# A linear attention followed by two MLPs on one core: a written-out order for the opening and the first block, and three chunks' y written from ScalarE's queue

## The chip, the core and the metric

One core of a Trainium2 chip runs the whole program. The metric is the device time in microseconds (us) of one execution. TensorE (PE) multiplies matrices into the eight PSUM banks, VectorE (DVE), ScalarE (ACT) and GpSimd (POOL) work element by element, and DMAs move data between HBM and SBUF. Every engine takes its own instructions in a fixed order and waits on semaphores for the others; a DMA is issued from the queue of an engine too, here always from SyncE's (SP) before the change.

## The reference, cut to what matters

```
B, H, S, D = 4, 8, 768, 48
for t in range(S):                                   # per batch and head
    state = alpha[t][:, None] * state + outer(k[t], v[t])
    y[t]  = q[t] @ state
x = y as (3072 tokens, 384)
x = (h * sigmoid(1.702 * h)) @ w_out,    h = x @ w_in        # 384 -> 2048 -> 384
x = (h - tanh(h)) @ w2_out,              h = x @ w2_in       # the same sizes
```

The weights of the MLPs come as 64-bit floats and are turned into pairs of 32-bit numbers on the chip.

## The kernel before, in words

**Attention.** Tokens go in 24 chunks of 128 (six per batch). A chunk g is loaded by four or five DMAs (`a_load`), its decays are multiplied up by two scans on DVE (`a_scan`), its queries and keys are scaled by two DVE multiplications (`a_scale`), and then PE makes the scores in two halves (`a_scores`, L273: two halves of four heads), ACT copies them out of PSUM (L278, L286), POOL cuts them to the causal triangle (L283), and PE makes the output y (`a_out`: L302 what the state carries, L305 what the chunk's own scores give) and the change of the state (L312), which DVE adds up (L316, L317, L319). `a_guard` squares the decays on ACT for a check at the end. For the first eight chunks (`FULL = 8`) the triangle is POOL's and the scaling DVE's; for the later ones the triangle is DVE's mask and the scaling POOL's.

**From y to x.** `a_evac` copies y out of PSUM on ACT (L326), writes it to HBM with four DMAs (L331) and reads it back in another layout with one (L332), after which ACT rounds it to `xhi` (L333) and DVE (or POOL) takes the rest as `xlo` (L334).

**The MLPs.** Each runs in 6 blocks of 512 tokens, 16 steps m to a block. A step is nine matmuls of `gemm1` (L343), the activation (`sig_1`: ACT L357, DVE L358), a split of the result into two (`g_split`: ACT L361, DVE or POOL L362) and, three steps later, nine matmuls of `gemm2` (L350). The hidden values alternate between banks 3 and 4, so `gemm1` of step m+2 overwrites what `sig_1` of step m reads. The first block of the first MLP needs chunks 0 to 3, and beside it chunks 4 to 7 are computed, and so on: every block of the first MLP but the last carries four chunks of the next.

**Weights.** A weight tile m is loaded as 64-bit words into one of three buffers `raw` (L153), and converted by DVE in `w_bits` (L160, L161), `w_join` (L173) and `w_split` (ACT's copy L190, DVE's L191). `conv` takes one step of a pipeline of three tiles: it splits one, joins the next and takes the bits of the one after, and the load of tile m+3 follows the join of tile m, whose buffer it takes. In the first block of the first MLP every step needs a tile that has been converted.

**The order.** The program is written as a list and a scheduler, which has a model of the engines' times, reorders it and fixes each engine's order at build time. Nothing ties the opening's order before the change.

**What the change touches:** `a_out` (L289), `a_evac` (L321), `conv` (L416), `attend` (L440), the opening (L455 to L475), and in the main loop the part for the first block (L493 to L511).

## Time and profile before

| | us |
|---|---|
| median of three runs | 974.35 (973.78 to 976.83) |
| the profiled execution | 975.3 |
| its span on the core | 973.2 |
| PE busy | 940.9 (97%) |
| DVE busy | 606.0 (62%) |
| ACT busy | 460.6 (47%) |
| POOL busy | 191.7 (20%) |

Times in the profile are counted from the start of the span; between that span and the profiled execution's own time lie 2.1 us outside it. "Busy" of PE counts matmuls whose ends are modelled and overlap, so that 97% doesn't mean that PE runs at its best. The granted share of TensorE's clock stands in the tables by stage; a matmul of 512 columns every 0.23 us is the clock's upper level (2.4 GHz), and one every 0.43 us the lower (1.2 GHz).

### The profile page before, as it was taken

Reading aid. Unit: us, or ns where it says so; the run is one execution under the profiler, and the core shown is the slowest. Engines: PE = TensorE matmul, PEld = TensorE weight load, DVE = VectorE, ACT = ScalarE, POOL = GpSimd, SP = SyncE. Lnnn points to the kernel's source line nnn. Section 1 sums busy time; section 2 is a strip of 40 time slices with the busy share of each in tenths; the row PEclk is TensorE's granted clock in tenths of the full one; section 3 lists DMA queues with packets and bytes.
Section 4 is the critical chain, followed back from the end, with each engine's and each line's share of the span. In section 5 each row is a group of like instructions: output and inputs, shape, how many; then the busy total and the mean of one; then the engine's idle time right before and its main releaser. Section 6 shows DMA issues by size and latency. Waiting matters only on the chain.

```text
span 973.2 us, 13227 instructions
## 1 busy us (share of the span) xinstructions
PE 940.9 (97%) x4870; PEld 739.7 (76%) x4870; DVE 606.0 (62%) x914; ACT 460.6 (47%) x969; POOL 191.7 (20%) x150
## 2 busy tenths in 40 slices
PE   5968999999999999999999999999999999999997
PEld 4646787777777777777788888888888888888885
DVE  7989742442343453453339996766777777766663
ACT  4445434333443534434344555554556656545542
POOL 1222202434434434334230110100100101000000
PEclk9999999999999999999999999999999999999999
DMA  9795221432445463761324330100233420000001
GB/s 282 245 305 166 85 53 28 131 92 67 137 141 153 151 205 116 247 196 41 92 71 158 134 130 1 65 33 0 70 126 98 161 100 0 33 1 1 33 0 37
DMA packets 58043, 101.84 MB, mean 105 GB/s; under 512 B 4992, under 2 KB 37376, under 8 KB 57968
## 3 DMA queue, kind: packets, MB, share of 16 engines
q1 hardware_dynamic: 57968, 100.90, 32.6%
q8 instruction: 40, 0.66, 0.3%
q14 instruction: 35, 0.29, 0.1%
HBM read 86.73 MB, written 14.16 MB: 104 GB/s over the span
## 4 chain that ended last, share of the span: by engine, by line
PE 87%; DMA 5%; DVE 5%; issue 1%; ACT 1%; SPq 0%; POOL 0%; DVEq 0%; ACTq 0%
PE bank L350 40%; PE bank L343 40%; DMA arena<-xq 4%; PE bank L273 3%; PE bank L305 2%; DMA raw<-w 2%; DVE arena L237 1%; PE bank L302 1%; PE bank L312 1%; DVE cf L161 1%; DVE cf L173 1%; DVE wlo L191 0%; DVE cf L160 0%; DVE xs L173 0%; ACT arena L248 0%
## 5 line engine op out<-in xcount | busy, mean ns | idle before, releaser
L343 PE MATMUL bank<-xhi,whi 128*128 128x512 f32 x576 | 230.0, 400 | 0.2 <-ACT xhi L333 0.2
L343 PE MATMUL bank<-xlo,whi 128*128 128x512 f32 x576 | 229.8, 399 | 0.0
L343 PE MATMUL bank<-xhi,wlo 128*128 128x512 f32 x576 | 229.0, 398 | 0.0
L350 PE MATMUL bank<-ghi,whi 128*128 128x512 f32 x576 | 229.0, 398 | 0.0
L350 PE MATMUL bank<-ghi,wlo 128*128 128x512 f32 x576 | 228.5, 397 | 0.0
L350 PE MATMUL bank<-glo,whi 128*128 128x512 f32 x576 | 223.8, 396 | 0.0
L361 ACT CAST ghi<-gt 128x512 fp32r<-128x512 f32 x192 | 119.0, 620 | 199.2 <-DVE gt L373 124.1
L358 DVE SCALAR_TENSOR_TENSOR gt<-gt,bank 128x512 f32<-128x512 f32 x96 | 65.5, 682 | 125.8 <-ACT gt L357 122.7
L362 DVE TENSOR_TENSOR glo<-gt,ghi 128x512 fp32r<-128x512 f32 x128 | 93.2, 728 | 79.4 <-ACT ghi L361 76.0
L343 PEld LDWEIGHTS bank<-xhi,whi 128*128 128x128 f32 x576 | 109.0, 189 | 27.4 <-issue 1.6
L343 PEld LDWEIGHTS bank<-xlo,whi 128*128 128x128 f32 x576 | 109.1, 189 | 26.2 <-issue 1.4
L343 PEld LDWEIGHTS bank<-xhi,wlo 128*128 128x128 f32 x576 | 109.2, 190 | 25.7 <-issue 0.6
L350 PEld LDWEIGHTS bank<-ghi,whi 128*128 128x128 f32 x576 | 108.5, 188 | 26.4 <-issue 1.2
L350 PEld LDWEIGHTS bank<-ghi,wlo 128*128 128x128 f32 x576 | 108.5, 188 | 25.4 <-issue 0.8
L350 PEld LDWEIGHTS bank<-glo,whi 128*128 128x128 f32 x576 | 108.3, 188 | 25.1 <-DVE arena L243 0.2
L362 POOL TENSOR_TENSOR glo<-gt,ghi 128x512 fp32r<-128x512 f32 x64 | 85.8, 1341 | 139.0 <-ACT ghi L361 127.8
L410 POOL TENSOR_TENSOR xlo<-arena,xhi 128x512 fp32r<-128x512 f32 x18 | 27.9, 1574 | 307.6 <-ACT xhi L409 307.6
L357 ACT ACTIVATE gt<-bank 128x512 f32<-128x512 f32 x96 | 57.1, 595 | 64.0 <-PE bank L343 63.1
L237 DVE TENSOR_TENSOR_SCAN arena<-arena,seg 112x516 f32<-112x516 f32 x46 | 62.8, 1365 | 35.4 <-DMA arena<-xq 34.7
L371 DVE SCALAR_TENSOR_TENSOR arena<-arena,bank 128x512 f32<-128x512 f32 x96 | 65.7, 685 | 30.4 <-ACT arena L369 29.7
L369 ACT ACTIVATE arena<-bank 128x512 f32<-128x512 f32 x96 | 57.3, 597 | 42.2 <-PE bank L343 41.9
L373 DVE SCALAR_TENSOR_TENSOR gt<-arena 128x512 f32<-128x512 f32 x96 | 68.3, 711 | 9.4
(85 smaller groups left out, 853.7 us busy)
## 6 DMA issues: line engine op xcount, KB each, us to landing
raw<-w SPq DMA_DIRECT2D x64, 768.0 KB, 4.7
arena<-xq SPq DMA_DIRECT2D x46, 224.0 KB, 3.0
arena<-xq SPq DMA_DIRECT2D x22, 451.5 KB, 5.8
xt<-arena SPq DMA_DIRECT2D x96, 48.0 KB, 3.0
xlo<-xt SPq DMA_DIRECT2D x24, 192.0 KB, 4.1
x1t<-xs SPq DMA_DIRECT2D x6, 768.0 KB, 5.2
arena<-x1t SPq DMA_DIRECT2D x6, 768.0 KB, 4.6
out<-xs SPq DMA_DIRECT2D x18, 256.0 KB, 2.3
```

The costliest lines, as they stand in the source:

```text
L237: V.tensor_tensor_scan(out=dec(g, n), data0=src(g, n), data1=seg, initial=0.0, op0=ALU.mult, op1=ALU.max)
L273: P.matmul(out=o[hh][:, i], lhsT=k[r, 2 * x + i], rhs=q[r, 2 * x + i], start=True, stop=True)
L343: P.matmul(out=h, lhsT=w[m][:, ws], rhs=x[:, k, :n], start=c == 0, stop=c == 3 * KT - 1)
L350: P.matmul(out=acc[k][:, :n], lhsT=w[m][:, ws], rhs=x[s % 3][:, :n], start=m == 0 and c == 0, stop=m == MT - 1 and c == 2)
L357: A.activation(out=th[i][:, :n], in_=h, func=AF.Tanh, scale=0.851)
L358: V.scalar_tensor_tensor(out=gf[i][:, :n], in0=th[i][:, :n], scalar=1.0, in1=h, op0=ALU.add, op1=ALU.mult)
L361: A.copy(ghi[s % 3][:, :n], gf[s % 2][:, :n])
L362: e.tensor_tensor(out=glo[s % 3][:, :n], in0=gf[s % 2][:, :n], in1=ghi[s % 3][:, :n].bitcast(F32), op=ALU.subtract)
L369: A.activation(out=u, in_=h, func=AF.Square, accum_out=usum[:, s - NS1 :][:, :1])
L371: V.scalar_tensor_tensor(out=p, in0=u, scalar=P3, in1=h, op0=ALU.mult, op1=ALU.mult)
L373: V.scalar_tensor_tensor(out=gf[i], in0=w, scalar=PD, in1=p, op0=ALU.add, op1=ALU.mult)
L410: G.tensor_tensor(out=xlo[i][:, k], in0=xr[:, k], in1=xhi[i][:, k].bitcast(F32), op=ALU.subtract)
```

## The change

It fixes the order of every engine's instructions (and of every queue's DMAs) from the first one to the end of the first block of the first MLP: `in_order` ties each instruction to the one written before it on the same engine. With that, the list itself is written anew. What moves:

- Loads: chunk 2 goes ahead of weight tiles 0 and 1, chunk 3 and tile 2 come after chunk 0's y, and a weight load is put off (`due`) to a `fetch()` behind the chunk's work.
- The opening runs chunk after chunk: the scores of chunk g, the scans and the scaling of chunk g+1, at most one step of `conv`, then y and the state of chunk g. Five steps of `conv` are taken ahead of the first block.
- The rounding of x (`a_x`) of chunk g comes two chunks later; y and its way back (`a_back`) are apart from it.
- For the first four chunks, `a_out` adds what the state carries after the chunk's own part instead of before it; y lies in banks 0 and 1, the scores in banks 5, 6, 3 and 4.
- y has a second buffer, which shares memory with `wt`. The y of chunks 1, 2 and 3 is written by DMAs from ACT's queue, the others from SP's.
- In the first block, `conv` and the weight load come ahead of the chunk's part of a step and `sig_1` after it; chunk 4+i takes steps 3i, 3i+1 and 3i+2.

```diff
+        early = g < L1[0][1] // C
+        if c and not early:
+            carried(True)
         for p, hh in heads:
...
+        if c and early:
+            carried(False)
...
     def a_evac(g, b):
+        ys = ysb[g % 2 if g < FULL else 0]
...
-                SP.dma_start(out=xt[2 * n + hh :: 4, :, tk].rearrange("h d t -> d h t"), in_=y4[64 * n : 64 * n + D, hh])
+                (A if 0 < g < L1[0][1] // C else SP).dma_start(out=xt[2 * n + hh :: 4, :, tk].rearrange("h d t -> d h t"), in_=y4[64 * n : 64 * n + D, hh])
+        if g >= FULL:
+            a_back(g)
+            a_x(g)
...
+    def a_back(g):
...
         SP.dma_start(out=xl[:, :, o].bitcast(F32), in_=xt.rearrange("h d t -> (h d) t")[:, tk].rearrange("(k p) t -> p k t", p=128))
+
+    def a_x(g):
+        xh, xl, o = a_at(g)
         A.copy(xh[:, :, o], xl[:, :, o].bitcast(F32))
         (V if g < FULL else G).tensor_tensor(out=xl[:, :, o], in0=xl[:, :, o].bitcast(F32), in1=xh[:, :, o].bitcast(F32), op=ALU.subtract)
...
             if m + 3 < MT:
-                w_load(layer, m + 3)
+                due.append((layer, m + 3))
...
+    def a_done(g, b=5):
+        a_evac(g, b)
+        if g + 2 < NG:
+            a_load(g + 2)
+        if g < FULL:
+            a_back(g)
...
+    def in_order(since):
+        last = {}
+        for ins in nc.cur_bb.bb.instructions[since:]:
+            if ins.engine in last:
+                tc.add_manual_dep(ins, last[ins.engine], mybir.DependencyInfo(
+                    mybir.DependencyClass.NoSync, mybir.DependencyReason.DATA), reason="in_order")
+            last[ins.engine] = ins.name
...
     a_load(1)
+    a_load(2)
+    w_load(1, 0)
+    w_load(1, 1)
+    for b in (0, 1, 7):
+        V.memset(bank[b], 0.0)
...
+    for r in range(3):
+        prep(0, r)
+    for g in range(4):
+        if g > 1:
             conv(1)
+        for r in range(2):
+            a_scores(g, r, (5, 3)[r])
+        if g < 3:
+            for r in range(3):
+                prep(g + 1, r)
+        else:
+            prep(4, 0)
+            prep(4, 1)
+        if g == 1:
+            conv(1)
+        if g > 1:
+            a_x(g - 2)
+        a_guard(g)
+        a_out(g, 0)
+        a_state(g)
+        a_evac(g, 0)
+        if g < 2:
+            a_load(g + 3)
+        if g == 0:
+            w_load(1, 2)
+        fetch()
+        a_back(g)
+    conv(1)
+    a_x(2)
+    a_x(3)
+    fetch()
+    a_load(5)
+    conv(1)
+    prep(4, 2)
+    prep(4, 3)
...
-            if l == 1:
+            if l == 1 and j:
                 sig_1(s, h, n)
-            else:
+            elif l == 1:
+                conv(1)
+                fetch()
...
+                    todo = ((4 * (m // 3) + m % 3,) if m % 3 < 2 else (4 * (m // 3) + 2, 4 * (m // 3) + 3)) if m < 12 else ()
+                for r in todo:
                     attend(t1 // C + r // 4, r % 4)
             if l == 1 and j == 0:
-                conv(1)
+                sig_1(s, h, n)
+                if m % 3 == 2 and m < 12:
+                    a_done(m // 3 + 4)
+                    a_state(m // 3 + 4)
+                    prep(m // 3 + 5, 3)
+                if m % 3 == 1 and m > 3:
+                    a_x(m // 3 + 3)
...
+        if s == MT - 1:
+            in_order(begin)
```

## Rows read from the trace of the kernel before

**Rows 1.** Stages: length; busy PE, PEld, DVE, ACT, POOL; clock, DMA share, GB/s.

```profile
0.00:65.50 65.50, 46.33 (x304) 34.34 (x305) 57.29 (x86) 29.17 (x79) 14.20 (x14) 1.00 0.89 274
65.50:83.00 17.50, 13.17 (x63) 9.26 (x63) 17.50 (x28) 9.05 (x21) 2.87 (x2) 0.81 0.81 259
...
150.35:234.01 83.66, 83.66 (x529) 64.62 (x528) 31.48 (x56) 31.83 (x71) 33.63 (x27) 1.00 0.32 92
624.41:691.33 66.92, 66.92 (x289) 54.26 (x288) 46.29 (x65) 34.45 (x70) 4.45 (x4) 1.00 0.10 36
```

**Rows 2.** PE in order of time: the first matmul of block 0, and of block 1.

```profile
65.50 0.80 PE L343 MATMUL bank<-xhi,whi 128*128 128x512 f32 x1 [0.18 <-ACT xhi L333]
...
150.35 0.39 PE L343 MATMUL bank<-xhi,whi 128*128 128x512 f32 x1
```

**Rows 3.** The chain of waits up to 100 us: start, length, what.

```profile
19.95 11.16 DMA arena<-xq
...
45.91 8.71 DMA raw<-w
```

**Rows 4.** PE in order of time in the opening: start, length, instructions.

```profile
8.72 4.05 PE L273 MATMUL bank<-arena 48*128 48x176 f32 x16 [8.72 <-ACT arena L218]
...
21.44 1.55 PE L273 MATMUL bank<-arena 48*128 48x176 f32 x8
...
59.32 1.28 PE L312 MATMUL bank<-arena 128*48 128x48 f32 x16
62.33 1.11 PE L302 MATMUL bank<-arena,state 48*48 48x128 f32 x16 [1.73 <-DVE state L317]
63.37 1.95 PE L305 MATMUL bank<-arena 128*48 128x128 f32 x16
```

**Rows 5.** Groups by line, ACT to 65.4 us, POOL to 110: busy us, mean ns.

```profile
L278 ACT COPY arena<-bank 128x256 f32<-128x256 f32 x20 | 7.6, 378 | 10.1 <-PE bank L305 6.3 <-PE bank L273 3.8
...
L283 POOL TENSOR_SCALAR_AFFINE_SELECT arena<-arena 128x512 f32<-128x512 f32 x14 | 21.7, 1555 | 78.5 <-ACT arena L278 72.2 <-ACT arena L286 6.3
```

**Rows 6.** POOL in order of time: two selects, one after the other.

```profile
44.95 5.60 POOL L283 TENSOR_SCALAR_AFFINE_SELECT arena<-arena 128x512 f32<-128x512 f32 x2 [6.99 <-ACT arena L278]
```

**Rows 7.** SP's queue in order of time: one chunk's y and its read back.

```profile
107.75 1.81 SPq L331 DMA_DIRECT2D xt<-arena  x4
110.92 0.40 SPq L332 DMA_DIRECT2D xlo<-xt  x1
```

**Rows 8.** ACT in order of time: the rounding that waits for that read.

```profile
113.37 0.52 ACT L333 CAST xhi<-xlo 128x384 fp32r<-128x384 f32 x1 [1.51 <-DMA xlo<-xt]
```

**Rows 9.** DVE in order of time, with no idle time between these.

```profile
84.13 1.22 DVE L237 TENSOR_TENSOR_SCAN arena<-arena,seg 112x516 f32<-112x516 f32 x1
85.27 0.53 DVE L160 TENSOR_SCALAR cf<-raw 128x768 int32<-128x768 int32 x1
85.73 0.55 DVE L160 TENSOR_SCALAR xs<-raw 128x768 int32<-128x768 int32 x1
86.19 0.68 DVE L362 TENSOR_TENSOR glo<-gt,ghi 128x512 fp32r<-128x512 f32 x1
86.80 0.67 DVE L358 SCALAR_TENSOR_TENSOR gt<-gt,bank 128x512 f32<-128x512 f32 x1
87.39 0.94 DVE L191 TENSOR_TENSOR wlo<-xs,whi 128x768 fp32r<-128x768 f32 x1
...
88.35 0.66 DVE L243 TENSOR_TENSOR arena<-arena 112x512 f32<-112x512 f32 x1
88.93 0.95 DVE L161 SCALAR_TENSOR_TENSOR cf<-raw,cf 128x768 int32<-128x768 int32 x1
89.80 0.95 DVE L161 SCALAR_TENSOR_TENSOR xs<-raw,xs 128x768 int32<-128x768 int32 x1
```

**Rows 10.** DMA issues up to 66 us: count, KB each, median us to landing.

```profile
raw<-w SPq DMA_DIRECT2D x12, 768.0 KB, 8.1
...
xt<-arena SPq DMA_DIRECT2D x17, 48.0 KB, 4.7
```

More of the change, by code (lines that the diff above doesn't have):

```diff
@@ L82, in linear_attention_mlps @@
     raw = [T(f"raw{i}", (128, WC, 2), I32) for i in range(3)]
-    wt = [T(f"wt{i}", (128, WC), mybir.dt.int16) for i in range(2)]
+    wtb = T("wtb", (128, WC))
+    wt = [wtb[:, i * WC // 2 : (i + 1) * WC // 2].bitcast(mybir.dt.int16) for i in range(2)]
     wsum = T("wsum", (128, 2 * MT))
@@ L296, in at, with carried @@
             return y[hh][64 * (p % 2) : 64 * (p % 2) + D, p // 2]
-        if c:
+        def carried(start):
             for p in range(NP):
@@ L301, in a_out @@
                     r = slice(64 * hh, 64 * hh + D)
-                    P.matmul(out=at(p, hh), lhsT=state[r, p], rhs=q[r, p, :C], start=p < 2, stop=False)
+                    P.matmul(out=at(p, hh), lhsT=state[r, p], rhs=q[r, p, :C], start=start and p < 2, stop=not start and p >= 2)
+        early = g < L1[0][1] // C
+        if c and not early:
+            carried(True)
         for p, hh in heads:
@@ L305, in a_out @@
             P.matmul(out=at(p, hh), lhsT=vt(g)[:, p, D * hh : D * hh + D], rhs=s4[:, hh, p % 2],
-                     start=not c and p < 2, stop=p >= 2)
+                     start=(early or not c) and p < 2, stop=not (c and early) and p >= 2)
+        if c and early:
+            carried(False)
         if c < NCH - 1:
@@ L313, in a_out, with a_state @@
                              start=True, stop=True)
+            if g >= FULL:
+                a_state(g)
+    def a_state(g):
+        c = g % NCH
+        if c < NCH - 1:
+            dl = bank[7][:DP, : NP * D].rearrange("p (a e) -> p a e", a=NP)
             al = dec3(g + 1, 0)[:, :, C:].to_broadcast([DP, NP, D])
@@ L414, in linear_attention_mlps, with fetch @@
     cv = [0, 0, 0]
+    due = []
+    def fetch():
+        while due:
+            w_load(*due.pop(0))
     def conv(layer, split=True):
@@ L443, in attend @@
         if r < 2:
-            a_scores(g, r, (b0, b1)[r])
+            a_scores(g, r, b)
         if r == 2:
-            a_out(g, b0)
-        if r:
+            a_out(g, b)
+        if 0 < r < 3 or r == 3 and g >= FULL:
             prep(g + 1, r)
-        if r == 3:
-            a_evac(g, b0)
-            for n in {0: (3,), 1: (4,), 2: ()}.get(g, (g + 2,)):
-                if n < NG:
-                    a_load(n)
+        if r == 3 and g >= FULL:
+            a_done(g, b)
+    def in_order(since):
[5 more added lines that the diff above has]
+            last[ins.engine] = ins.name
+    begin = len(nc.cur_bb.bb.instructions)
     V.memset(seg, A_MIN)
@@ L506, in linear_attention_mlps @@
                 t1, n1 = L1[j + 1]
-                parts, span = n1 // C * 4, 11
-                for r in range(min(parts, -(-m * parts // span)), min(parts, -(-(m + 1) * parts // span))):
+                if j:
+                    parts, span = n1 // C * 4, 11
+                    todo = range(min(parts, -(-m * parts // span)), min(parts, -(-(m + 1) * parts // span)))
+                else:
+                    todo = ((4 * (m // 3) + m % 3,) if m % 3 < 2 else (4 * (m // 3) + 2, 4 * (m // 3) + 3)) if m < 12 else ()
+                for r in todo:
                     attend(t1 // C + r // 4, r % 4)
             if l == 1 and j == 0:
-                conv(1)
+                sig_1(s, h, n)
[5 more added lines that the diff above has]
+                    a_x(m // 3 + 3)
             if 2 <= j < 4 and m % 2:
```

32 lines of the change are left out of this document (13 added, 19 removed).

## The prediction

> **What bounds the kernel now.** I read the table by stage first. From about 83 us on, PE is busy without a gap; a block of the second MLP, which has nothing but its matmuls, takes 66.92 us, and block 1 of the first MLP, which carries four chunks of attention beside the same matmuls, 83.66 us [rows 1]. So a step of matmuls (half a sixteenth of 66.92, one `gemm` of nine) is 2.09 us, and a chunk costs PE (83.66 - 66.92) / 4 = 4.2 us. From block 1 on PE is the bound, and nothing of the change lies there. The change lies in the first 150.35 us, up to block 1's first matmul [rows 2]. Of these, 65.5 pass before block 0's first matmul, and block 0 takes 84.85, against what PE needs for it: 16 `gemm1`, 13 `gemm2` (the last three fall into block 1) and four chunks, 29 x 2.09 + 16.7 = 77.4 us. So 7.5 us are lost in block 0, and whatever of the 65.5 can be saved comes on top.
>
> Then I asked what bounds the opening. DVE is busy 57.3 of the first 65.5 us and all of the next 17.5, PE 46.3 of the 65.5, and DMA engines 0.89 of it at 274 GB/s [rows 1]. The chain of waits goes through loads that took 11.16 us (a chunk's) and 8.71 us (a weight tile's) [rows 3], because chunks and weight tiles share the bandwidth, and otherwise through DVE's conversions. Those conversions run many weight tiles ahead, while block 0's first matmul needs one tile. So the opening is late because work that could wait stands ahead of work that can't.
>
> **The change part by part.** *The opening's chain.* In the new order PE may start the scores of chunk g+1 only after all of `a_out(g)`. The period of a chunk is then a chain: two halves of scores, 1.55 us each; ACT's two copies of the second half, 2 x 0.38; POOL's select of it, 1.56 in the mean; the chunk's own part of y 1.95, the carried part 1.11, the state's 1.28 [rows 4, 5]. The sum is 9.8, but modelled ends run past the next start (L302 starts at 62.33, L305 at 63.37, which is 1.04 and not 1.11 [rows 4]), with some 0.1 to 0.2 in each of five groups of PE: I take 9.0. Bounds: 8.2 with the select at half its mean, and 10.7 with selects of 2.8 us, as in the pair that took 5.60 [rows 6]. DVE needs less per chunk (next part but one: 3.6 of scans and scaling, at most 3.1 of conversion, 1.0 of smaller ones), so that PE, ACT and POOL's chain sets the pace. The first scores start at 8.72 us [rows 4], which stays: constants and chunk 0 are still the first loads, and two more memsets of DVE fall into its wait for them. Chunk 3's y is complete at 8.72 + 4 x 9.0 - 1.28 = 43.4. From there to x: two copies 0.8, and 5.6 us from the first DMA of y to the rounding (107.75 to 113.37, in a stretch with little traffic [rows 7, 8]). Block 0's first matmul (T0) comes at 43.4 + 0.8 + 5.6 + 0.5 = **50.3**, between 47 and 57, against 65.5. I take 50.
>
> *The loads.* Chunk 2 ahead of tiles 0 and 1, chunk 3 behind chunk 0's y on SP. At 274 GB/s [rows 1], chunks 0 to 2 (1.1 MB each by the sizes of their arrays) and two tiles (0.8 MB each [rows 10]) are 5 MB and are in by about 20 us, chunk 3 by about 25; its scans come at 27 to 31. I cost the move at nothing, covered by that margin of some 2 us; without it, the opening is late by what is missing.
>
> *ACT issues y of chunks 1, 2 and 3.* No DMA was issued from ACT's queue before, so the price is bounded: four issues take SP 1.81 us [rows 7]. If ACT is held as long, what stands behind is the copy of the next chunk's first scores, and that waits for PE anyway: state part 1.28 and scores 1.55 after the same point. I take 0; the bounds are 0 and 4 us over three chunks (half of SP's time again, and nothing hidden), and a gain of up to 1 us each, since SP is free to hold the loads and reads. The Trainium skill, "DMA: Bandwidth & Descriptors" (section "Issuing engines are not separate DMA queues"), says that issuing from several engines saves the sequencer's issue time alone; by that too the move gives nothing on the wire, and the sum stays.
>
> *Block 0: DVE is next.* What was not converted ahead must now be converted inside block 0, and this is where the saving ends. From the starts of DVE's instructions in a stretch without a gap [rows 9]: a scan 1.14, the two int operations 0.46 and 0.87, the split 0.87, a scaling 0.58, `glo` and `sig_1`'s part 0.6 each; the join is of the same kind and size as L161, 0.87. So a full `conv` is 3.08 us, a chunk's scans and scaling 3.6 (two scans, two scalings, 0.15 of small ones), and the three small operations of a chunk (two of 192 elements and one of 384, against L243's 512) at most 1.0 together. After chunk 3's x, DVE has, up to `sig_1` of step 11: twelve `conv` and the last join and split, 38.7; scans and scaling of four chunks and the rest of one, 15.6; small ones 4; twelve `sig_1` 7.2 and eleven `glo` 6.6. The sum is **72 us for twelve steps**, against PE's 12 `gemm1`, 9 `gemm2` and four chunks, 43.9 + 16.7 = 61. So DVE is the bound of the first twelve steps. Step 13's `gemm1` waits for step 11's `sig_1` (same bank): 50 + 72 = 122. Then PE has three `gemm1` and three `gemm2` to block 1's first matmul, 12.5 us: 134.5. DVE will not be without idle time in an order where every engine waits in line (the split waits for ACT's copy, which stands behind the `tanh` before it, which waits for PE): 0 us idle as between 65.5 and 83, or 12% as in the opening's 57.3 of 65.5 [rows 1], which on 72 is 9. I take 5.5: **block 1 begins at 140**, against 150.35, 10.4 us earlier.
>
> *Behind.* From block 1 on the scheduler still orders freely, with the same work: 0, and plus or minus 2.5 for another draw of its list.
>
> **The sum.** 975.3 for the profiled execution less 10.4 is 964.9; the profiled one stood 0.95 above the median of 974.35, so the forecast is **964.0**. Its own bounds: T0 at 47 and no idle gives 47 + 72 + 12.5 = 131.5, that is 18.9 earlier, 955.5; T0 at 55 and 8 idle gives 147.5, 971.5.
>
> **The rivals.** *A: more than that.* PE rather than DVE bounds block 0 if DVE's conversions run further ahead in the opening (DVE has some 10 us idle there): 50 + 77.4 = 127.4 and 2 us lost, 20 us earlier, near 954. For it: PE waits for nothing else. Against it: the written order puts only five `conv` ahead. Chance 0.14.
>
> *B: no change to speak of (within 0.3%, 2.9 us, which is about what a measurement of this kernel can tell).* The opening's chain takes 10.7 us per chunk and T0 is 57, and 8 us of idle time follow: 149.5, that is 973.5. What decides is POOL's select: it now stands on the chain once per chunk, beside a DVE that is never empty. The pair of 5.60 us ran while DVE converted; the mean of fourteen is 1.56 [rows 5, 6]. The Trainium skill, "SBUF — State Buffer" (section "SBUF: two separate sides"), has a lock for this: DVE and GpSimd share a pair of ports that one of them holds for a whole instruction while the other is blocked. This trace agrees as far as the spread goes; by that rule every select could be a long one. A drop of PE's clock belongs here too: between 65.5 and 83, with PE busy 13.2 of 17.5, the granted share was 0.81 [rows 1], 3.4 us of PE's time; in the new order PE idles about one part in seven of each step, and each drop of that kind eats idle time first. Chance 0.13, with the case that the scheduler's order was already nearly this one (its loads of 11.16 us speak against it).
>
> *C: slower.* One mechanism: SP's queue in block 0. In every third step it holds, in line, y's four writes, a chunk's loads and the read of x, which waits until y has landed; the next weight load stands behind. That load has two steps, 12 us, until its bits are wanted. In quiet traffic the hold is 3.2 us (107.75 to 110.92 [rows 7]) and a load's landing less than 8.1, and it fits. With landings as in the old opening, 8.1 for a weight tile and 4.7 for y [rows 10], hold and landing come to 1.8 for y's issues, 4.7, as much as y's 1.8 for the chunk's four loads, and 8.1, which is 16.4, and DVE stands still for 4 us per chunk, 16 in all. Then block 1 begins at 134.5 + 5.5 + 16 = 156, 5.6 later than before: 980. It comes out slower by over 0.3% from a delay of 3.4 us per chunk on (13.3 in all, 10.4 of gain and 2.9). Against it: block 0's traffic is some 16 MB in 80 us, 200 GB/s, less than the 274 of the old opening. Chance 0.12.
>
> **How the numbers follow.** Forecast 0.61, A 0.14, B 0.13, C 0.12. The forecast's own bounds of 955.5 to 971.5 lie wholly on the faster side of 971.4, but for its edge. Faster: 0.61 + 0.14 = 0.75; same: 0.13; slower: 0.12. The range leaves out C and a part of A: 955 to 975.
>
> **What would show it.** The first L343 at 47 to 55 us and block 1's at 135 to 147. DVE near full from T0 for 70 us, then half empty; PE with gaps of about 1 us per step up to step 11 and none after. Four chunks' `a_out` at a spacing of 8.2 to 10 us. No load on the chain of waits before 45 us. ACT's four issues within 2.5 us. I am wrong where L160 waits for `raw` in block 0 for more than 5 us in sum (C), where L305 waits for L283 by more than 2 us per chunk (B), or where PE's granted share stays low beyond 60 us.

## The result, and the profile after

The changed kernel takes 979.51 us (978.74 to 981.70) beside 974.67 us (973.78 to 976.83) of the kernel before: a ratio of 1.0054 with a 95% interval of 1.0040 to 1.0069. It is slower by half a per cent, where 964.0 was forecast, in a range of 955 to 975. Its profiled execution took 979.44 us, its span 977.8 us (973.2 before).

In the rows of after, line numbers have moved: `gemm1` is L370 (L343 before), `gemm2` L377, the bits L161 and L162 (L160, L161), the join L174, ACT's copy of the split L191 and DVE's part L192, `sig_1`'s DVE part L385, `glo` L389, the guard's square L249, the copy of y L338, its writes L343 and its read back L356.

Stages of after, with the columns of [rows 1]: the opening; block 0 up to the end of `sig_1` of step 11; the rest of block 0; block 1.

```profile
0.00:50.57 50.57, 25.67 (x240) 19.82 (x240) 36.27 (x56) 21.10 (x62) 7.64 (x12) 1.00 0.79 225
50.57:135.01 84.44, 74.66 (x430) 55.56 (x431) 76.54 (x107) 36.93 (x87) 12.68 (x10) 0.92 0.55 171
135.01:152.47 17.46, 16.21 (x78) 12.35 (x78) 14.08 (x23) 6.67 (x15) 4.60 (x3) 1.00 0.42 116
152.47:234.00 81.53, 81.53 (x507) 63.39 (x506) 31.07 (x54) 32.08 (x69) 33.42 (x26) 1.00 0.32 92
```

PE of after in order of time, the two rows that answer to [rows 2]: the first matmul of block 0 and of block 1.

```profile
50.57 0.80 PE L370 MATMUL bank<-xhi,whi 128*128 128x512 f32 x1 [6.96 <-ACT xhi L360]
...
152.47 0.39 PE L370 MATMUL bank<-xhi,whi 128*128 128x512 f32 x1
```

The opening gained what it was to gain: T0, the first matmul of block 0, is at 50.57 where 50 was forecast, 14.9 us earlier than before. Block 0 then takes 101.9 us where 90 was forecast and 84.85 were needed before, so block 1 begins at 152.47, later than the 150.35 of before. From there to the end it takes 825.3 us against 822.9, but another execution of the kernel before takes 825.5 (e0, below), so these 2.4 us are no more than two executions of one kernel differ by. The loss is in block 0, and its parts are these:

| from T0 to block 1 | forecast | after | before |
|---|---|---|---|
| DVE's work up to `sig_1` of step 11 | 72 | 76.5 | 57.9 |
| DVE idle in that time | 5.5 | 7.9 | 12.3 |
| from there to block 1 | 12.5 | 17.5 | 14.7 |
| sum | 90 | 101.9 | 84.9 |

(Before, half of block 0's conversions had been done in the opening; that is why its DVE had less to do.) That DVE is what block 0 waits for up to there shows in PE's idle time. PE sits idle five times in that stretch, 9.8 us in all, and each time starts again within 0.11 us of the end of an operation of DVE: `sig_1`'s part once, the scaling of the next chunk (L245) four times. Three of these waits, 7.4 us, the profile puts down to nothing that it sees ("issue"), as here (DVE, then PE):

```profile
73.68 0.68 DVE L245 TENSOR_TENSOR arena<-arena 112x512 f32<-112x512 f32 x1
```

```profile
74.47 1.55 PE L274 MATMUL bank<-arena 48*128 48x176 f32 x8 [2.69 <-issue]
```

And that stretch is 84.42 to 84.46 us long in all six kernels that share block 0's tied order (after, and e3, e7, e11, e12 and e13 below), at granted clocks of 0.87 to 0.92.

Nearly all of DVE's idle time (7.2 of 7.9 us) has one cause. The list of its waits in that stretch of after has a single entry, with the columns total us, times, longest us:

```profile
DVE wlo L192 <- ACT whi L191: 7.2, 4, 1.9
```

How that wait comes about is seen on the two engines. ACT in order of time, then DVE:

```profile
70.41 0.64 ACT L338 COPY arena<-bank 112x256 f32<-112x256 f32 x2
75.66 1.06 ACT L249 ACTIVATE arena<-arena 112x1032 f32<-112x1032 f32 x1 [4.61 <-DVE state L331]
76.63 0.19 ACT L249 ACTIVATION_READ_ACCUMULATOR arena<-arena 112x1 f32 x1
76.72 0.82 ACT L191 CAST whi<-cf 128x768 fp32r<-128x768 f32 x1
```

```profile
75.26 0.36 DVE L331 TENSOR_TENSOR state<-state,arena 112x192 f32<-112x192 f32 x1
77.57 0.96 DVE L192 TENSOR_TENSOR wlo<-cf,whi 128x768 fp32r<-128x768 f32 x1 [1.95 <-ACT whi L191]
```

This is a loop through two engines' lines. The guard of the next chunk squares a chunk's decays in place, so it must wait until DVE has read them for the last time (here the state step L331; in the other cases the state step L333 or the scaling L245). In ACT's tied line it stands ahead of the copy L191, which the next split needs and which had nothing else to wait for. DVE comes to that split straight after and finds that ACT has only begun its square. DVE stands 1.94, 1.95, 1.35 and 1.94 us, and DVE is the bound there. Three of the four waits come from `prep(m // 3 + 5, 3)`, written behind `a_state` in every third step; the first (at 57.7 us) is the same thing with chunk 4's guard, which the list has at the end of the opening (`prep(4, 3)`).

The rest of block 0 was undersized in the forecast by 2.2 us even for the kernel before (14.7 against 12.5): PE has seven `gemm`s left there and not six (63 matmuls without a pause, four `gemm2` and three `gemm1`). In after PE has six left, but beside them come 2.9 us of scores and state part of chunk 8, which the tail of before doesn't hold, and 1.3 us of idle time. On the chain of waits there stands another wait of DVE:

```profile
135.32 0.36 DVE L331 TENSOR_TENSOR state<-state,arena 112x192 f32<-112x192 f32 x1
138.66 1.23 DVE L238 TENSOR_TENSOR_SCAN arena<-arena,seg 112x516 f32<-112x516 f32 x1 [2.99 <-DMA arena<-xq]
139.81 0.93 DVE L192 TENSOR_TENSOR wlo<-cf,whi 128x768 fp32r<-128x768 f32 x1
...
141.09 1.24 DVE L389 TENSOR_TENSOR glo<-gt,ghi 128x512 fp32r<-128x512 f32 x1
...
142.59 0.67 DVE L385 SCALAR_TENSOR_TENSOR gt<-gt,bank 128x512 f32<-128x512 f32 x1
```

The scan at 138.66 is chunk 9's, which block 1's list wants; the ties end with block 0, and the scheduler put it, with its wait for a load, ahead of the last split and of `sig_1` of step 12.

### The profile page after: what moved, and what is told of

It is laid out like the page before. It is cut to its first block, busy times and chain, and to the rows that moved or that the text cites. A ratio compares the mean times of both kernels' runs of the same rounds, so it can differ in the third digit from the quotient of the medians.

```text
span 977.8 us, 13190 instructions
## 1 busy us (share of the span) xinstructions
PE 933.6 (95%) x4870; PEld 732.4 (75%) x4870; DVE 613.5 (63%) x916; ACT 459.6 (47%) x969; POOL 190.8 (20%) x150
## 4 chain that ended last, share of the span: by engine, by line
PE 87%; DMA 4%; DVE 4%; issue 1%; ACT 1%; SPq 1%; ACTq 0%; POOL 0%; DVEq 0%; POOLq 0%
PE bank L377 40%; PE bank L370 40%; PE bank L274 3%; PE bank L310 2%; DMA arena<-xq 2%; PE bank L303 1%; DMA xlo<-xt 1%; DMA raw<-w 1%; DVE arena L238 1%; PE bank L319 1%; DVE wlo L192 1%; DVE glo L389 1%; DVE xs L174 0%; ACTq L343 0%; DVE gt L385 0%
## 5 line engine op out<-in xcount | busy, mean ns | idle before, releaser
L370 PE MATMUL bank<-xhi,whi 128*128 128x512 f32 x576 | 232.3, 403 | 8.6 <-ACT xhi L360 7.0
L370 PE MATMUL bank<-xhi,wlo 128*128 128x512 f32 x576 | 231.1, 401 | 0.0
L370 PE MATMUL bank<-xlo,whi 128*128 128x512 f32 x576 | 230.8, 401 | 0.0
L377 PE MATMUL bank<-ghi,whi 128*128 128x512 f32 x576 | 230.8, 401 | 0.0
L377 PE MATMUL bank<-ghi,wlo 128*128 128x512 f32 x576 | 229.6, 399 | 0.0
L377 PE MATMUL bank<-glo,whi 128*128 128x512 f32 x576 | 225.5, 398 | 0.0
L385 DVE SCALAR_TENSOR_TENSOR gt<-gt,bank 128x512 f32<-128x512 f32 x96 | 65.4, 681 | 123.3 <-ACT gt L384 123.1
L389 DVE TENSOR_TENSOR glo<-gt,ghi 128x512 fp32r<-128x512 f32 x128 | 93.2, 728 | 74.2 <-ACT ghi L388 70.2
L370 PEld LDWEIGHTS bank<-xhi,whi 128*128 128x128 f32 x576 | 109.9, 191 | 37.1 <-ACT xhi L360 7.1
L370 PEld LDWEIGHTS bank<-xlo,whi 128*128 128x128 f32 x576 | 109.9, 191 | 27.1 <-issue 1.4
L370 PEld LDWEIGHTS bank<-xhi,wlo 128*128 128x128 f32 x576 | 109.8, 191 | 26.9 <-issue 0.6
L377 PEld LDWEIGHTS bank<-ghi,whi 128*128 128x128 f32 x576 | 108.8, 189 | 28.0 <-issue 2.7
L377 PEld LDWEIGHTS bank<-ghi,wlo 128*128 128x128 f32 x576 | 109.0, 189 | 26.1 <-issue 0.8
L377 PEld LDWEIGHTS bank<-glo,whi 128*128 128x128 f32 x576 | 108.9, 189 | 26.0 <-issue 0.6
L389 POOL TENSOR_TENSOR glo<-gt,ghi 128x512 fp32r<-128x512 f32 x64 | 87.1, 1362 | 117.7 <-ACT ghi L388 108.1
```

The source lines that it names most:

```text
L370: P.matmul(out=h, lhsT=w[m][:, ws], rhs=x[:, k, :n], start=c == 0, stop=c == 3 * KT - 1)
L377: P.matmul(out=acc[k][:, :n], lhsT=w[m][:, ws], rhs=x[s % 3][:, :n], start=m == 0 and c == 0, stop=m == MT - 1 and c == 2)
L385: V.scalar_tensor_tensor(out=gf[i][:, :n], in0=th[i][:, :n], scalar=1.0, in1=h, op0=ALU.add, op1=ALU.mult)
L389: e.tensor_tensor(out=glo[s % 3][:, :n], in0=gf[s % 2][:, :n], in1=ghi[s % 3][:, :n].bitcast(F32), op=ALU.subtract)
```

## The experiments

**The same kernel again, and the list without its ties.** e0 is the kernel before, unchanged; e1 is the changed kernel without the call of `in_order`.

```diff
-        if s == MT - 1:
-            in_order(begin)
```

> The kernel before, unchanged, profiled beside the experiments. The last blocks took 66.92 us each in its first profile and 67.20 in the changed kernel's. If that belongs to the chip, they take 67.1 to 67.3 here too; if it belongs to the change, 66.9. Block 3 (84.4 before, 91.4 after) stays at 84 to 86 in either case.

> The changed kernel without the ties of in_order: the new list, the scheduler's freedom as before. Theory 1 (block 0 went from 84.9 to 101.9 us because each engine waits in line): block 0 falls to 84 to 92, the first matmul lies at 50 to 62, 966 to 974 us in all. Rival (block 0 is long because only five steps of conversion stand ahead of it, in whatever order): block 0 stays at 96 or more, 975 to 982. Rival for the later part (block 3's 6.9 us are a draw of the scheduler's list): block 3 takes another value, 84 to 87 as likely as 91.

e0: 975.46 us; T0 65.17, block 0 82.95, block 3 84.4 and the last blocks 66.92 again, but block 4 88.45 where the execution of [rows 1] had 86.01. A stage of one execution is good to some 2 us. e1: 974.93 us, ratio 1.0002 (0.9983 to 1.0022), T0 at 67.87, block 0 82.3: neither the theory nor the rival. Without the ties the rewritten list changes nothing: the scheduler makes the old opening from it. All that the change does, it does by the ties.

**Ties in the opening only.** `in_order(begin)` is called ahead of the main loop and not behind block 0.

```diff
+    in_order(begin)
     steps = [(1, j, m) for j in range(len(L1)) ...
...
-        if s == MT - 1:
-            in_order(begin)
```

> The ties of in_order end with the opening; block 0 is the scheduler's. Theory 1: the first matmul stays at 50 to 52 us, block 0 falls to 88 to 95, 967 to 974 us. Rival (DVE's work itself bounds block 0, with 72 to 76 us of it up to step 11): block 0 stays at 97 to 102, 975 to 980.

971.36 us, ratio 0.9975 (0.9953 to 0.9996). T0 is 50.12 and block 0 takes 95.4 instead of 101.9, 0.4 above the theory's range: DVE idles 4.1 us instead of 7.9, and the tail is 2.1 shorter. So the ties in block 0 cost about 6.5 us there, and those in the opening are worth having.

**SP writes all of y.**

```diff
-                (A if 0 < g < L1[0][1] // C else SP).dma_start(...)
+                SP.dma_start(...)
```

> The changed kernel with all of y's writes issued by SP. ACT's issues of chunk 1 took from 23.7 to 30.1 us and held the next chunk's copies back by about 6 us. If that is ACT's own wait and the loads could have gone on meanwhile: the first matmul comes at 45 to 49, the end 1 to 4 us earlier if block 0 were not DVE's. If block 0's DVE line decides, the end gains no more than 4 and no less than 0: 975 to 980. Rival: on SP the same issues hold the loads of chunk 4 and the read of chunk 1 back; the first matmul at 51 to 56.

974.96 us, ratio 1.0004 (0.9986 to 1.0021), 4.5 us less than with the change, and T0 at 46.07, 4.5 earlier. What I had costed at 0 costs 2.7 to 4.5: block 1 begins only 3.1 us earlier, since the tail of block 0 is 1.4 longer, and over all kernels here with that tied opening T0 lies at 49.2 to 50.6 where ACT issues y (after, e2 and e4 to e7) and at 46.1 to 48.1 where SP does (e3 and e8 to e10), 2.7 us in the mean. ACT in order of time with the writes on its queue, the kernel after:

```profile
22.04 0.65 ACT L338 COPY wtb<-bank 112x256 f32<-112x256 f32 x2 [2.17 <-PE bank L303]
23.65 6.42 ACTq L343 DMA_DIRECT2D xt<-wtb  x4
30.17 0.65 ACT L279 COPY arena<-bank 128x256 f32<-128x256 f32 x2 [7.48 <-DMA xt<-wtb]
```

and the same place with them on SP's, e3:

```profile
21.93 0.65 ACT L338 COPY wtb<-bank 112x256 f32<-112x256 f32 x2 [2.17 <-PE bank L303]
24.25 0.65 ACT L279 COPY arena<-bank 128x256 f32<-128x256 f32 x2 [1.68 <-PE bank L274]
```

Chunk 1's four issues hold ACT for 6.42 us (6.0 to 7.2 in e2 and e4 to e7), and the copy of chunk 2's scores, which stands at 24.25 in e3, comes at 30.17. Chunk 2's and 3's issues take 1.83 and 2.90 us and do little. The cover that I had named (state part and scores) is there, but it is 1.7 us, not 6.4.

The Trainium skill, "DMA: Bandwidth & Descriptors" (section "Issuing engines are not separate DMA queues"), says that issuing from several engines saves only sequencer time. That the move brings nothing on the wire agrees with these runs; that the issuing engine can lose by it is what e3 shows (T0 4.5 us earlier with SP issuing).

**Chunk 4's load behind chunk 1's read back.** My first explanation was bandwidth: SP, freed of y, issues chunk 4's load ahead of chunk 1's y, and the two share the DMA engines. e11 is the changed kernel with that load moved.

```diff
-        if g < 2:
-            a_load(g + 3)
         if g == 0:
+            a_load(3)
             w_load(1, 2)
         fetch()
         a_back(g)
+        if g == 1:
+            a_load(4)
```

> The changed kernel with chunk 4's load put behind chunk 1's read back in SP's line; ScalarE still issues y of chunks 1 to 3. Theory: the 6.42 us that ScalarE spends on chunk 1's four issues (23.65 to 30.1 in the changed kernel), and the 7.48 us for which it is late there, come from chunk 4's load, which SP, freed of y, issues ahead (from 21.80 on) and with which y then shares the DMA engines. Then ScalarE's four issues take 3 to 4 us here, block 0's first matmul stands at 46 to 47 (50.57 in the changed kernel, 46.07 where SP issues y), and the kernel takes 974 to 976. Rival: an issue from ScalarE's line is slow by itself, or behind chunk 2's load and the read back of chunk 0: the four issues still take over 5 us, the first matmul stands at 49.5 or later, and the kernel takes 978 to 980.

978.85 us, ratio 1.0061 (1.0040 to 1.0081), T0 48.84: between the two forecasts, and the total at the rival's. ACT in order of time, e11:

```profile
22.31 2.81 ACTq L343 DMA_DIRECT2D xt<-wtb  x4
25.21 0.65 ACT L279 COPY arena<-bank 128x256 f32<-128x256 f32 x2 [2.66 <-issue]
...
31.45 2.68 ACTq L343 DMA_DIRECT2D xt<-arena  x4
34.18 0.83 ACT L191 CAST whi<-cf 128x768 fp32r<-128x768 f32 x1 [2.48 <-DMA arena<-xq]
```

Chunk 1's issues are down to 2.81 us, as the theory had it, but now chunk 2's hold ACT, behind the load that was moved there. And the 1.7 us gained at T0 were lost again, twice over, in the tail of block 0 (21.1 us instead of 17.5), where PE idled and then ran in part at the clock's lower level (a granted share of 0.65 and 0.66; after has 1.00 in its tail, where DVE's wait for chunk 9's load is 3.0 us and not 3.7):

```profile
140.00:145.00 5.00, 4.09 (x17) 3.11 (x18) 4.95 (x9) 1.99 (x5) 2.25 (x2) 0.65 0.15 31
145.00:150.00 5.00, 5.00 (x17) 3.93 (x16) 5.00 (x8) 1.60 (x4) 1.81 (x2) 0.66 0.10 32
```

**Number of transfers or bytes.** The chain of waits of after, around chunk 1's y (start, length, what), gave the better idea:

```profile
21.37 8.37 DMA xlo<-xt
29.73 0.02 issue
29.75 0.32 ACTq L343
30.08 0.04 issue
```

ACT's last issue begins 0.02 us after chunk 0's read back has landed, and the one before it 0.03 us after weight tile 2, with which y has nothing to do. Counted back among the issues of all queues, each is the eighth before. Among the 312 DMAs of each of before, after, e3 and e11 an issue never begins before the eighth issue ahead of it has landed, and 11 to 18 per trace begin within 0.1 us after that landing. Counting seven back, 20 to 32 issues per trace begin too early; counting nine back, none begins close behind the landing. e12 adds four loads of 1 KB to e11, behind chunk 0's read back and ahead of chunk 1's y, into a buffer that nothing reads: four issues more and next to no bytes. e13 is e11 with chunk 2's y on SP.

```diff
         a_back(g)
+        if g == 0:
+            for i in range(4):
+                SP.dma_start(out=tiny[:, 4 * i : 4 * i + 4], in_=cst[:16, 4 * i : 4 * i + 4])
```

```diff
-                (A if 0 < g < L1[0][1] // C else SP).dma_start(...)
+                (A if g in (1, 3) else SP).dma_start(...)
```

> The kernel of the run with chunk 4's load behind (e11), with four loads of 1 KB each (16 by 16 elements into a buffer that nothing reads) issued by SP after chunk 0's read back and ahead of chunk 1's y. They add next to nothing to what the DMA engines move. Theory A (count): in every trace so far the issue of a DMA, on whatever queue, never comes before the DMA eight issues earlier has landed (312 DMAs, no exception), and ScalarE's third and fourth issue in the changed kernel began 0.03 and 0.02 us after such a landing. With four more issues between, ScalarE's third and fourth issue for chunk 1 have to wait for weight tile 2 and for chunk 0's read back, which landed at 27.08 and 27.79: the four issues take 5 to 6 us, the copy of the next scores comes at about 28.2 instead of 25.21, and block 0's first matmul at 50.5 to 52.5. Theory B (bandwidth): issues are late where the DMA engines are full; 4 KB change nothing, the four issues take 2.5 to 3.3 us, and the first matmul stands at 48 to 49.5.

> The kernel of the run with chunk 4's load behind (e11), with chunk 2's y issued by SP; chunks 1 and 3 stay with ScalarE. Theory A (count): what that run lost against SP's issuing all of them (first matmul at 48.84 against 46.07) is chunk 2's fourth issue, which waited for the landing of chunk 4's first load, eight issues earlier, and held ScalarE to 34.1. With that on SP the first matmul comes at 46 to 47.2. Theory B: an issue from ScalarE's line is slow by itself, whatever is under way (2.81 us for chunk 1's four): then about 1 us is lost at chunk 1 and another at chunk 3, and the first matmul comes at 47.7 to 49. The total follows it, at 974 to 976 or 976 to 978.5, and the table's spread of 2 us may hide that.

e12, ACT in order of time:

```profile
24.23 4.15 ACTq L344 DMA_DIRECT2D xt<-wtb  x4
28.47 0.65 ACT L280 COPY arena<-bank 128x256 f32<-128x256 f32 x2 [5.57 <-DMA xlo<-xt]
```

and e13:

```profile
21.98 2.02 ACTq L343 DMA_DIRECT2D xt<-wtb  x4
24.10 0.65 ACT L279 COPY arena<-bank 128x256 f32<-128x256 f32 x2 [1.87 <-PE bank L274]
```

In e12 the first of the four has to wait too (the copy of y before it ends at 22.9; from there the issues take 5.5 us), the third and fourth begin at 27.54 and 28.05, 0.02 us after weight tile 2 (27.52) and the read back (28.03) have landed, and the next copy comes at 28.47 instead of 25.21. T0 is 50.25, 0.25 us below the range of theory A and 0.75 above that of B; its one execution took 977.44 us. In e13 ACT's four issues take 2.02 us, the copy behind them waits for PE as in e3, T0 is 46.76, and the time is 975.70 us, ratio 1.0012 (0.9994 to 1.0030). So the count decides, and an issue from ACT's queue is not slow by itself. What the change does is to move waits which held only SP's loads into the line of an engine that has other work behind them. The limit is in the program as it is built. In every trace the DMAs tell of their landing on the same eight semaphores, used in turn, so that a DMA has that of the eighth one ahead of it (save where the issues of two queues cross). In all sixteen traces, 236 issues begin within 0.1 us of the landing of the eighth one ahead, and every one of them waits for just that semaphore, by itself or by an instruction right before it in its queue. Whether the chip would bear more transfers under way, no run tells. My first explanation, bandwidth, falls.

**The guard out of the loop.** The guard of chunk 4 + i moves one step later, behind `sig_1`.

```diff
                     a_done(m // 3 + 4)
                     a_state(m // 3 + 4)
-                    prep(m // 3 + 5, 3)
+                if m % 3 == 0 and 0 < m < 13:
+                    prep(m // 3 + 4, 3)
```

> The changed kernel, with the square of the next chunk's decays on ACT put one step later in block 0. Theory: four of DVE's waits of 1.4 to 1.9 us each (first split of every third step, behind ACT's copy, behind this square, which waits for DVE's own state) are a loop through ACT's line; they go, 7 us less idle time, block 0 at 94 to 97, 973 to 976 us. Rival: the same wait comes back behind ACT's next instruction in line, the copy of y: block 0 above 99.

969.55 us, ratio 0.9944 (0.9924 to 0.9964): 10 us less than with the change, by moving one activation per chunk, and 3.5 below the theory's range. The list of DVE's waits in the same stretch, e5 (the one that is left is chunk 4's guard, which this edit leaves where it was; I had counted it among the four that would go):

```profile
DVE wlo L192 <- ACT whi L191: 1.9, 1, 1.9
```

ACT, then DVE in the step that stood above (all 0.8 us earlier):

```profile
70.37 0.84 ACT L191 CAST whi<-cf 128x768 fp32r<-128x768 f32 x1
...
76.04 1.09 ACT L249 ACTIVATE arena<-arena 112x1032 f32<-112x1032 f32 x1
```

```profile
74.51 0.36 DVE L331 TENSOR_TENSOR state<-state,arena 112x192 f32<-112x192 f32 x1
74.78 0.95 DVE L192 TENSOR_TENSOR wlo<-cf,whi 128x768 fp32r<-128x768 f32 x1
```

ACT has made the copy 3.6 us before DVE wants it, and DVE goes from L331 to L192 without a pause. Block 0 takes 93.78 us: DVE's line is 5.8 us shorter and the tail 2.3 (15.2; the split and `glo` now stand ahead of the scan, which waits 1.5 us). The loop is shown as the cause of the waits; that the tail came right with it is what this run shows, and why the scheduler then chose another order is not. Of the 12.0 us by which e5's profiled execution is shorter than that of after, 0.8 lie ahead of T0, 8.1 in block 0 and 3.1 behind block 1's start, where nothing was changed.

**`glo` on POOL in block 0.** DVE is the bound there, so taking eleven operations off it should help, if nothing else.

```diff
-                prev = s - 1, n, V if l == 2 or j in (0, len(L1) - 1) else G
+                prev = s - 1, n, V if l == 2 or j == len(L1) - 1 else G
```

> The changed kernel, with the subtraction that makes glo in block 0 moved from DVE to POOL, which is busy 10 of block 0's first 76 us. Theory 1 (DVE's line is what block 0 waits for): it takes 7.1 us off DVE's 84.4 up to step 11's sig_1, block 0 falls from 101.9 to 94 to 97, 973 to 976 us in all. Rival (PE or the later loads bound block 0): within 2 us of 101.9. Rival (POOL and DVE hold each other up, 1.36 us per subtraction on POOL): 100 or more.

979.17 us, ratio 1.0050 (1.0033 to 1.0067), and block 0 at 104.6: the second rival. DVE's line in block 0 is 86.8 us instead of 84.4 although it has eleven operations less. Groups by line up to `sig_1` of step 11 (busy us, mean ns, idle before), POOL and DVE of e4:

```profile
L389 POOL TENSOR_TENSOR glo<-gt,ghi 128x512 fp32r<-128x512 f32 x11 | 24.7, 2249 | 46.0 <-ACT ghi L388 46.0
...
L162 DVE SCALAR_TENSOR_TENSOR cf<-raw,cf 128x768 int32<-128x768 int32 x7 | 10.2, 1455 | 0.2
L174 DVE SCALAR_TENSOR_TENSOR cf<-raw,cf 128x768 int32<-128x768 int32 x7 | 8.8, 1262 | 0.0
```

and DVE of after:

```profile
L162 DVE SCALAR_TENSOR_TENSOR cf<-raw,cf 128x768 int32<-128x768 int32 x7 | 7.6, 1092 | 0.2
L174 DVE SCALAR_TENSOR_TENSOR cf<-raw,cf 128x768 int32<-128x768 int32 x7 | 6.6, 948 | 0.0
```

POOL takes 2249 ns for a `glo`, against 1362 over the whole of after (x64, all beside a less busy DVE), and DVE's bits and joins get a third longer. The Trainium skill, "SBUF — State Buffer" (section "SBUF: two separate sides"), has DVE and GpSimd lock each other out of a shared pair of ports, with a GpSimd operation that reads SBUF and a DVE operation with two SBUF inputs among the pairs that collide; by that both sides pay, and this trace agrees (1455 against 1092 ns, 2249 against 1362).

**The two operations of the bits apart.** DVE's L162 reads what L161 has just written. e6 puts the join of another tile between the two.

```diff
+        todo = cv[0] < min(layer * MT, cv[2] + len(cfs[layer]))
+        if todo and layer == 1:
+            w_bits(layer, cv[0] % MT, 0)        # the first of the two
         ... w_join(layer, m) ...
-        if cv[0] < min(layer * MT, cv[2] + len(cfs[layer])):
-            w_bits(layer, cv[0] % MT)
+        if todo:
+            w_bits(layer, cv[0] % MT, 1 if layer == 1 else 2)
```

> The changed kernel, with the join put between the two operations of w_bits for the first MLP. Theory: the second, which reads what the first has just written, starts 0.6 us after it instead of the 0.46 seen between independent ones, and the pair takes 1.64 us instead of 1.33; twelve pairs are 3.7 us, block 0 at 97 to 99, 975.5 to 978 us. Rival: the pair's length comes from POOL or from the operands, and nothing changes: 101 to 103.

976.61 us, ratio 1.0030 (1.0013 to 1.0047). Block 0 takes 100.4 us, between the theory's range and the rival's. DVE's line of block 0 is 82.7 us instead of 84.4, and DVE is busy 1.5 us less of it, so about a third of the 4.5 us by which its work was undersized are such pauses between dependent operations. The rest goes with POOL, as the rival had it in part. POOL, then DVE, of after:

```profile
64.86 1.37 POOL L284 TENSOR_SCALAR_AFFINE_SELECT arena<-arena 128x512 f32<-128x512 f32 x1 [5.68 <-ACT arena L279]
```

```profile
65.77 1.27 DVE L162 SCALAR_TENSOR_TENSOR cf<-raw,cf 128x768 int32<-128x768 int32 x1
...
71.60 0.96 DVE L162 SCALAR_TENSOR_TENSOR cf<-raw,cf 128x768 int32<-128x768 int32 x1
```

Of the twelve L162 in that stretch of after, the four that run beside an operation of POOL take 1.27 us and the other eight 0.96. Three L161 take 0.99 instead of 0.55, one join 1.39 instead of 0.95 and one `glo` 1.67 instead of 0.68, all of them beside POOL: 4.0 us together, a little more than what is left to explain, so other operations were priced somewhat high. No run took the selects away; e4, with more of POOL beside DVE, shows the same from the other side.

**The ties into block 1**, so that the untied scan can't get ahead:

```diff
-        if s == MT - 1:
+        if s == MT + 2:
             in_order(begin)
```

> The changed kernel, with the ties going on through step 2 of block 1. Theory: the 5 us that block 0's end lost against the estimate (17.5 us from step 11's sig_1 to block 1 instead of 12.5) come from block 1's instructions that the scheduler put between the tied ones, of them a scan that waits 3 us for chunk 9: block 0 at 96 to 99, block 1 then up to 2 longer, 976 to 979 us. Rival: the end is bound by the tied instructions themselves: block 0 at 101 or more.

992.22 us, ratio 1.0168 (1.0139 to 1.0197). Block 0 is at 98.8, as the theory had it, with a tail of 14.35 us instead of 17.46 that holds no work of chunk 8 and no idle time of PE; but block 1 takes 98.85 us instead of 81.53, where up to 2 more were expected. DVE's waits in block 1 of e7:

```profile
DVE gt L385 <- ACT gt L384: 28.5, 10, 5.8
DVE arena L238 <- DMA arena<-xq: 20.6, 3, 9.0
```

The longest of these waits, 9.0 us for a chunk's load, ends at 182.3 us, a third of the way into block 1 and behind the last tie; the three tied steps themselves take 21.1 us instead of 15.6. So a longer tied start moves the seam, and what the scheduler makes of the rest of the block is dearer than the tail was; why it places the loads so late there was not followed further.

**Both losses removed**, the guard's move and SP for all of y (e8), the same with the bits apart (e9), and ties in the opening only with SP for all of y (e10):

> The changed kernel with both: y's writes all on SP, and the square of the next chunk's decays one step later in block 0. Theory (two losses that have nothing to do with each other: 4.5 us of the opening, in ACT's issues, and 8 us of block 0, in the loop through ACT's line): first matmul at 46, block 0 at 93 to 96, 964 to 967 us. Rival (block 0 gives back what the opening gains, since its conversions wait for loads): block 0 at 97 or more, 968 to 971.

> As the one above, and the join between the two operations of w_bits, which took 1.7 us off DVE's line by itself. If the three add up: block 0 at 91 to 94, 962 to 966 us. If PE's end of block 0 (15 us behind step 11's sig_1) or the loads bound it by now: no more than 1 us below the one above.

> The ties in the opening alone, with y's writes on SP; block 0 is the scheduler's, which had 95.4 us there with the writes on ACT. If the 4.5 us of the opening come through: first matmul at 45 to 47, block 0 at 94 to 97, 965 to 969 us. Rival (the scheduler's own model of the opening changes with the queue, and so does its block 0): block 0 at 99 or more, 971 to 975.

e8: 964.06 us, ratio 0.9896 (0.9878 to 0.9914), as its theory had it, with block 0 at 93.7. e9: 964.22 us, 0.9891 (0.9871 to 0.9911). e10: 969.69 us, 0.9946 (0.9928 to 0.9965), with T0 at 48.13 and block 0 at 95.6: time and T0 each lie just above the theory's ranges. Stages of e8, cut as those of after above:

```profile
0.00:47.01 47.01, 25.91 (x240) 19.80 (x240) 36.69 (x57) 21.30 (x62) 9.52 (x12) 1.00 0.87 250
47.01:125.61 78.60, 69.05 (x421) 52.02 (x422) 75.76 (x106) 37.84 (x88) 14.01 (x10) 0.91 0.60 179
125.61:140.67 15.06, 15.06 (x66) 12.01 (x65) 12.61 (x20) 6.03 (x11) 2.92 (x2) 1.00 0.46 119
140.67:224.84 84.17, 84.00 (x529) 64.72 (x528) 32.34 (x57) 31.99 (x71) 33.69 (x27) 1.00 0.32 92
```

Block 1 begins at 140.67, DVE is busy 75.76 of 78.60 us, and e8 is faster than both kernels, by 10 us than the one before and by 15 than the changed one (3.5 of these 15 lie behind block 1's start, 821.8 us against 825.3, where nothing was changed). e9 takes another 1.7 us off DVE's line (block 1 at 138.98), which doesn't show in its time.

## Why the prediction was wrong

**The bound was named rightly, and the total was wrong in the order's own waits and in two terms of block 0 that were too small.** DVE bounds block 0 in after as forecast: it is busy 76.5 of the 84.4 us up to `sig_1` of step 11, and PE's gaps follow it. The forecast's mechanism gives its time, 964, once two waits that the change brings along are taken out (e8). That the number is the same to 0.1 us is chance: e8's T0 is 3 us earlier than forecast, and its block 0 3.7 longer (DVE's work 3.8 and the tail 2.6 longer, idle time 2.7 shorter).

**Step by step.** Block 1 began 12.5 us later than the 140 of the sum: T0 0.6, DVE's work 4.5, DVE's idle time 2.4, the tail 5.0. The 2.4 behind block 1's start lie within the bound that was given for it, and within what two executions of before differ by.

*T0*: right by two errors that cancel. With SP writing y (e3), the carried part of chunk 3's y ends at 37.8 and not at 43.4: by the prediction's own formula a chunk takes (37.8 + 1.28 - 8.72) / 4 = 7.6 us, below the lower bound of 8.2. I had taken too little off the durations of [rows 4, 5] for what overlaps: in e3 the two halves of scores take 2.72 us together and not 3.1, the state's part 0.88 and not 1.28, and POOL's select 0.9 to 1.2 in the new opening (after, e3) and not 1.56. Nor does the upper bound come out of its words: selects of 2.8 us make it 9.0 + 1.24 = 10.2, not 10.7. Against these 5.6 us stand 4.5 of ACT's issues and a longer way from y to x (8.3 in e3, 6.9 forecast).

*ACT's issues of y*: the first step that failed, costed at 0 with an upper bound of 4, and 4.5 in e3 at T0 (2.7 in the mean of all kernels with that opening). The bound was made from the time that four issues take SP in a quiet stretch [rows 7], and by its own words (1.81 us, half again, three times, nothing hidden) it should have been 8.1. But an issue can also wait, in line, for a transfer issued eight places before, and in the opening eight transfers are under way. The trace of before has it too (no exception among its 312 issues, 18 close behind the landing), but I had not read it for that. The sign given in the prediction, four issues within 2.5 us, told it at once (6.42).

*Loads cost nothing*: held. DVE waits 2.8 us in sum for chunk loads in the opening. The sign I had named for it, no load on the chain of waits before 45 us, was a bad one: the chain runs through loads on which only the count of eight depends.

*DVE's idle time*: the second and dearer step that failed. I took 5.5 us from an average, between 0 and 12%, and so priced no wait at all. The wait that decided could be read from the diff and the program: in every third step, and once at the end of the opening, the guard stands in ACT's line ahead of the copy for the split and behind DVE's last reading of the decays. I had even named that copy as a place where DVE may wait, but with the `tanh` ahead of it, and not asked what else the tied order puts there. The size in idle time (7.9 against 5.5) looks small; taking three of the four waits away took 8.1 us off block 0 (e5), since the tail went with it.

*DVE's work*: 76.5 against 72. The pair of L160 and L161 was priced at 1.33 us from [rows 9], where the two operations on one tile are never neighbours: 0.46 was the distance between operations on two tiles. In the written order the second reads what the first has just written, and the pair takes 1.46 to 1.90; twelve of them cost 4.2 us more. e6, which takes them apart, gives 1.5 back. The rest are operations that run longer beside POOL (above); I had looked for that price on POOL's select only, in rival B, and found it on DVE.

*The tail*: the largest miss of the sum, 17.5 against 12.5. 12.5 was PE's time for six `gemm`s alone; the trace of before could have told seven and 14.7. What after has beyond that is the seam between a tied and a free order (the untied scan, and chunk 8's work), which the tail of e7 doesn't have; I had put such things under "behind", with ±2.5.

**The rivals.** A didn't come: DVE stays the bound. B's select is on the opening's chain but short (0.9 to 1.2 us each). By its letter the sign that I had named for B came: PE waits for the select 9.1 us in the opening of after, over 2 us a chunk. But 6.2 of these are chunk 2's, behind ACT's issues, and in e3 it is 4.0 in all. The clock did fall, to a granted 0.92 in block 0 (0.91 in e8), but DVE's stretch kept its length there (84.4 us at 0.87 to 0.92). C had the right sign and the wrong queue, and that its 980 is near the time measured is chance: no wait of L161 for `raw` is in the list of block 0, and it was ACT's line that held DVE and not SP's that held the loads. What C and the result have in common is the kind of thing: an instruction that waits in line, with work behind it that could go.

**What stays open.** Why block 3 takes 88.5 to 93.2 us in after, e2, e3, e6 and e10 to e13, and 84.43 in before, e0, e1, e4, e5, e8 and e9. The kernels of the first group also have a block 1 of 81.3 to 81.6 us and those of the second one of 83.6 to 84.2, so it seems to go with one of two orders that the scheduler makes of the rest. In after a chunk's load stands on the chain of waits in block 3; no run was made for it.

## What to carry to other kernels

When an order is tied by hand, go through each engine's line and ask of every instruction that waits for another engine what stands behind it, and whether that other engine will soon wait for it: three such waits of 1.3 to 2.0 us, with what followed from them, cost 8 us of block 0 here (e5). An idle allowance taken from an average is no price for a new order. A DMA's issue is an instruction that can wait; before it goes to a busy engine's queue, count what is under way at that place, and the semaphores that the program has for it, not only the time that an issue takes.

## What the runs showed of the hardware

A DMA issue, on SP's or ACT's queue, never began before the eighth issue ahead of it (over both queues) had landed: some 312 DMAs in each of sixteen traces without an exception, and four 1 KB loads put in between moved ACT's next copy from 25.21 to 28.47 us (e12). Where an issue came right behind such a landing it was the program that waited, for one of its eight landing semaphores (236 of 236 issues); a limit of the chip's own isn't shown.

The steady blocks of the second MLP, 288 matmuls of 512 columns, take 66.92 us in before, e0, e1, e4, e5, e8, e9 and e12, and 67.20 in after, e2, e3, e6, e7, e10, e11 and e13, that is 232.4 or 233.3 ns a matmul, in two runs of the same job on one chip as well. It goes with the build and not with the order of block 0: e12 differs from e11 only by its four small loads and their buffer. From block 5 on it is worth 1.95 us (475.59 against 477.54 us to the last matmul), which is most of the 2.4 us between before and after behind block 1, and some of what e5 and e8 gain on it. Its cause is open.
